# Local attention with a gated feed-forward network on one core: where Wo's weights stand in their slots, where raw weights land, and when the halo is zeroed

## The chip, the cores and the metric

The kernel runs on one core of a Trainium2 chip. The metric is the device time of one launch in microseconds, the median of several runs of the same build. A core has five engines that are named here as the profile names them: PE (matrix multiply, with PEld for its weight loads), DVE, ACT, POOL and SP. SP and POOL also issue the DMA transfers of this kernel.

## The reference, cut to what matters

One sequence of 2048 tokens with 640 features is layer-normalised to `xn`. Two branches are computed from `xn` and multiplied:

```
qkv  = xn @ wqkv                 # 640 -> 3 * 640, 32 heads of 20
o    = softmax(q . k over the tokens s, s-2, ..., s-14) . v
s    = o @ wo                    # 640 -> 640
g    = silu(silu(xn @ w1) @ w2)  # 640 -> 1536 -> 640
out  = x + s * g
```

Everything is float32.

## The kernel before, in words

**Groups.** The 2048 tokens are worked off in four groups of 512 (`NG` = 4, `T` = 4 tiles of `P` = 128 tokens). A group runs through `qkv_phase` (four quarters of the heads, each 3 x 160 columns), then, for the group before it, `wo_phase`, then `ffn_phase`. After the last group stands `wo_last`. The attention itself (`scores`, `values`) runs on DVE beside the matrix products of the phases that follow.

**Two halves of each number.** Each float32 operand is held as a rounded half and the rest (`TH`/`TL` for the normalised and transposed activations, `SH`/`SL` for the inner activations of the feed-forward network, `whi`/`wlo` for weights). A product is three passes: high by high, high by low, low by high. Each matmul takes one 128x128 stationary operand, loaded by a weight load of its own, and one moving operand:

- q, k, v (lines 633 to 635, and 579 for the first quarter): stationary `TH`/`TL`, moving 480 columns of a weight slot.
- w1 (lines 786 to 788): stationary 128 columns of a weight slot, moving 512 columns of `TH`/`TL`.
- w2 (lines 667 and 669, through `tm_mm`): stationary `SH`/`SL`, moving 384 and then 256 columns of a weight slot.
- Wo (the same lines 667 and 669, and 756 in `wo_last`): stationary `TH`/`TL` (which then hold the transposed attention output), moving 384 and then 256 columns of a weight slot.

**Weight slots.** `WR` has seven slots (`RING` = 7) of 2 x 640 numbers, that is 5120 bytes in each partition. The list `units` holds the 196 weight blocks in the order of use; block i goes to slot i mod 7. `start(u)` gives the first column of a block in its slot: 48 (`QAT`) for the blocks of wqkv and 0 for the others. The high half begins there and the low half 640 numbers (2560 bytes) further on. When PE is done with a block, `w_done` calls `w_load` for the block seven places on.

**First use and reuse.** The first time a block is needed its raw float32 weights are loaded by SP (`raw_load`, line 345; the very first load is issued by ACT), ACT rounds them into the high half (line 371), and DVE, or POOL for the first ones, computes the low half (line 374). The two halves are stored to DRAM (line 380), and later uses load both by one DMA that POOL issues (line 363). Of the 57 raw loads the first five land in `PR`, the next ones, in turn, in six places of 2560 bytes (two tiles `RAW` and four parts of the gate tile `G`), and those of group 1 in the two `RAW` tiles.

**Residual.** `wo_phase` loads the input rows again, into the two tiles `XR` (line 705, SP); POOL adds the gated attention to them (line 706), and SP stores the result (line 708).

**Halo.** Each quarter has a tile `KV[q]` with 7 extra positions for keys and values of neighbouring tokens. In group 0, POOL zeroes the first two partitions of these positions by a memset (line 641), before SP's shifting DMAs (line 454) fill the rest.

**Order.** Nothing is issued as it is written. `add` records each operation with its engine, an estimated duration, the keys that it reads and writes, and a priority; `Weave.order` then lays all operations out, PE's in the written order and the other engines' by readiness and priority, and emits them. Each engine works off its own list in that order; SP's and POOL's DMA issues wait in the same list.

**Placement.** The tiles stand in each partition in the order of allocation. In the built program `TH`, `TL` and all seven slots begin at the same place modulo 512 bytes (`TH[0]` at 17152, `TL[0]` at 37632, the slots from 58112 in steps of 5120, each 256 modulo 512). The small tile `ST[1]` stands between the slots and `SH`, so that `SH` and `SL` begin 64 bytes later modulo 512.

Of the kernel before, what the change touches and what calls it, by code (L numbers as in the profile page):

```python
# [9 lines left out]
F32R = mybir.dt.float32r  # L10
# [4 lines left out]
P = 128  # L15
S, D, F, H, DH = 2048, 640, 1536, 32, 20
# [12 lines left out]
CA, CB = 384, 256  # L29
RING = 7  # L30
# [2 lines left out]
LO = 10  # L33
BY_ACT = (0,)
QAT = 48
X_AT = 3, 7, 8
TILE_AT = 1, 1.5, 5, 6
LOW_AT = 3
# [20 lines left out]
class Weave:  # L59
# [19 lines left out]
    def add(self, eng, dur, fn, reads=(), writes=(), prio=0.0, lock=False, table=None, nbytes=0):  # L79
        o = Op()  # L80
        o.eng, o.dur, o.fn, o.prio, o.lock, o.table, o.nbytes = eng, dur, fn, prio, lock, table, nbytes
        o.seq, o.users, o.ready = len(self.ops), [], 0.0
        before = set()
        for k in reads:
            if k in self.writer:
                before.add(self.writer[k])
        for k in writes:
            if k in self.writer:
                before.add(self.writer[k])
            before.update(self.readers.get(k, ()))  # L90
        for k in writes:
            self.writer[k] = o
            self.readers[k] = []
        for k in reads:
            self.readers.setdefault(k, []).append(o)
        before.discard(o)
        o.left = len(before)
        for b in before:
            b.users.append(o)
        self.ops.append(o)  # L100
        return o
# [71 lines left out]
def local_attention_silu_ffn(ctx: ExitStack, tc: tile.TileContext, x, wqkv, wo, w1, w2, out):  # L173
# [19 lines left out]
    def tiles(name, n, shape, dtype=F32):  # L193
        return [sb.tile(shape, dtype, name=f"{name}{i}") for i in range(n)]
# [4 lines left out]
    ST = [sb.tile([P, 2, 6], F32, name="st0")]  # L199
    TH = tiles("th", 2, [P, DC, TOK], F32R)  # L200
    TL = tiles("tl", 2, [P, DC, TOK], F32R)
    WR = tiles("w", RING, [P, 2 * D], F32R)
    ST.append(sb.tile([P, 2, 6], F32, name="st1"))
    SH = tiles("sh", 2, [P, TOK], F32R)
    SL = tiles("sl", 2, [P, TOK], F32R)
# [11 lines left out]
    G = sb.tile([P, T, D], F32, name="gate")  # L217
    XR = tiles("xr", 2, [P, D])
    SF = tiles("sf", 2, [P, TOK])
    RAW = tiles("raw", 2, [P, D])  # L220
    ACC = [psum.tile([P, TOK], F32, name=f"acc{i}") for i in range(6)]
    ROT = [psum.tile([P, TOK], F32, name=f"rot{i}") for i in range(2)]
    carry = [dram.tile([2, NQ, 2, T, CQ], F32, name=f"carry{par}") for par in range(2)]
# [8 lines left out]
    def bank():  # L232
        i = take("acc", 6)
        return ACC[i], ("acc", i)
# [14 lines left out]
    def act(n, fn, reads, writes, prio, table=None):  # L249
        add("ACT", ac(n), fn, reads, writes, prio, table=table)  # L250
# [5 lines left out]
    def dma(fn, reads, writes, nbytes, prio, dur=0.45):  # L256
        add("SP", dur, fn, reads, writes, prio, nbytes=nbytes)
# [37 lines left out]
    def store_at(u):  # L295

        return 1 + (u[0] == "q" and u[2] % 2)

    for u in units:
        n = seen[u] = seen.get(u, 0) + 1  # L300
        at = store_at(u)
# [5 lines left out]
    def width(u):  # L307
        return 3 * CQ if u[0] == "q" else D

    def start(u):  # L310

        return QAT if u[0] == "q" else 0

    def raw_load(k):


        if k >= len(fresh):
            return
        i = fresh[k]
        u = units[i]  # L320
        n = width(u)
        if k < DC:
            r, kr = PR.rearrange("p t w m -> p (t w m)")[:, k * n:(k + 1) * n], [PRK[k]]
        elif k < early:
            s = (k - DC) % 6
            r, kr = (RAW[s], [("raw", s)]) if s < 2 else (G[:, s - 2, :], [("g", s - 2, 0), ("g", s - 2, CA)])
            r = r[:, :n]
        else:
            s = k % 2
            r, kr = RAW[s][:, :n], [("raw", s)]  # L330
        raws[i] = r, kr
        if u[0] == "q":
            _, q, c = u
            src = wqkv[c * P:(c + 1) * P, :].rearrange("p (s m) -> p s m", s=3)[:, :, q * CQ:(q + 1) * CQ]
            dst = r.rearrange("p (s m) -> p s m", s=3)
        elif u[0] == "w1":
            src = w1.rearrange("(c p) f -> p c f", p=P)[:, :, u[1] * P:(u[1] + 1) * P]
            dst = r.rearrange("p (c f) -> p c f", c=DC)
        else:
            m = wo if u[0] == "wo" else w2  # L340
            src, dst = m[u[1] * P:(u[1] + 1) * P, :], r
        if k in BY_ACT:
            add("ACT", 0.65, lambda: nc.scalar.dma_start(dst, src), [], kr, -1, nbytes=n * P * 4)
            return
        dma(lambda: nc.sync.dma_start(dst, src), [], kr, n * P * 4, 1 + k if k < 2 * DC else clock[0] + 5,
            0.62 if k < 2 * DC else 0.45)

    def w_load():
        i = loaded[0]
        if i >= len(units):  # L350
            return
        loaded[0] += 1
        u, s = units[i], i % RING
        n = width(u)
        r = WR[s]
        at = start(u)
        both = r.rearrange("p (s d) -> p s d", s=2)[:, :, at:at + n]
        whi, wlo = both[:, 0], both[:, 1]
        kh, kl = ("wh", s), ("wl", s)
        due = clock[0]  # L360
        if what[i] == "load":
            src = halves[u]
            add("POOL", 1.0, lambda: nc.gpsimd.dma_start(both, src), [("half", u)], [kh, kl], due + 10,  # L363
                nbytes=2 * n * P * 4)
            return
        k = fresh.index(i)
        if not k:
            raw_load(0)
            rawn[0] = 1
        raw, kr = raws.pop(i)  # L370
        act(n, lambda: nc.scalar.activation(whi, raw, AF.Copy), kr if k else kr + [("sd", 0)], [kh], 1000 + due)
        pool_does = k < LO and k not in ON_DVE
        eng, cost, by = ("POOL", po(n), nc.gpsimd) if pool_does else ("DVE", dv(n), nc.vector)
        add(eng, cost, lambda: by.tensor_tensor(
            out=wlo, in0=raw, in1=whi.bitcast(F32), op=OP.subtract), [kh] + kr, [kl],
            due if pool_does else LOW_AT if k < LO else 50, lock=True)
        if what[i] == "store":
            kept = dram.tile([P, 2, n], F32, name="half_" + "_".join(map(str, u)))
            halves[u] = kept
            dma(lambda: nc.sync.dma_start(kept, both.bitcast(F32)), [kh, kl], [("half", u)], 2 * n * P * 4,  # L380
                due + 25)
        while rawn[0] <= (min(k + 6, early - 1) if k < early - 2 else k + 2):
            raw_load(rawn[0])
            rawn[0] += 1

    def w_next(*want):
# [4 lines left out]
        s, n, at = i % RING, width(want), start(want)  # L391
        return WR[s][:, at:at + n], WR[s][:, D + at:D + at + n], ("wh", s), ("wl", s)

# [5 lines left out]
    def load_x(g, t, n=1, prio=None):  # L399
        dma(lambda: nc.sync.dma_start(XIN[:, t:t + n], rows(xg, g)[:, t:t + n]), [],  # L400
            [("xin", u) for u in range(t, t + n)], n * P * D * 4, clock[0] if prio is None else prio)
# [124 lines left out]
    def first_quarter(i):  # L526
# [59 lines left out]
        for k in range(2):  # L586
            cs = slice(k * 320, (k + 1) * 320)
            dma(lambda cs=cs: nc.sync.dma_start(XIN[:, 0, cs], rows(xg, 0)[:, 0, cs]), [],
                [("xin", 0) if k else ("xin", 0, "a")], P * 320 * 4, 0)
        for k, p in enumerate(X_AT):  # L590
            load_x(0, k + 1, prio=p)
# [27 lines left out]
    def qkv_phase(g, i, io):  # L619
        for q in range(NQ):  # L620
            if g == 0 and q == 0:
                ps = first_quarter(i)
            else:
                ps = [bank() for t in range(T)]
                for c in range(DC):
                    wh, wl, kh, kl = w_next("q", q, c)
                    for t in range(T):
                        o, kp = ps[t]

                        def unit(c=c, t=t, o=o, wh=wh, wl=wl):  # L630
                            o = o[:, :3 * CQ]
                            hi, lo = TH[i][:, c, tsl(t)], TL[i][:, c, tsl(t)]
                            nc.tensor.matmul(o, hi, wh, start=c == 0, stop=False)  # L633
                            nc.tensor.matmul(o, lo, wh, start=False, stop=False)  # L634
                            nc.tensor.matmul(o, hi, wl, start=False, stop=c == DC - 1)  # L635
                        pe(3 * mm(480), unit, t_keys(i, [c], [t]) + [kh, kl], [kp])
                    w_done()
                    if g and (q, c) in O_AT:
                        o_chunk(g - 1, O_AT[q, c], io)
            if g == 0:  # L640
                add("POOL", 2.0, lambda q=q: nc.gpsimd.memset(KV[q][0:2, :, 0:HALO, :], 0.0), ["first"] if q else [],
                    [("halo", q, 1, 0), ("halo", q, 2, 0), ("halo", q, 3, 0), ("halo", q, 4, 0)], 1 + q)
            for t in range(T):
                evac_qkv(g, q, t, *ps[t])
            halo(g, q)
            scores(g, q)
            if q:
                values(g, q - 1)
        values(g, NQ - 1)
# [217 lines left out]
```

## Time and profile before

| | |
|---|---|
| median of 3 runs | 642.76 us (641.28 to 643.1) |
| the profiled execution | 641.45 us |
| its span, first to last instruction | 639.6 us |
| PE busy | 632.7 us (99%) |
| DVE busy | 538.7 us (84%) |
| ACT busy | 207.2 us (32%) |
| POOL busy | 123.4 us (19%) |
| HBM read, written | 109.55 MB, 34.16 MB |

Busy times are those of the profiled execution. Matmuls overlap each other in the records, since one begins before the last rows of the one before it are out; what a matmul costs PE is therefore read from start to start in the timeline, and the duration of one record is longer than that.

### The profile page before, as it was taken

The numbers are of one execution on the slowest core, as the hardware profiler recorded it, in microseconds if no ns is written. First come the engines' busy times: TensorE is split into PE (matmuls) and PEld (weight loads), VectorE is DVE, ScalarE is ACT, GpSimd is POOL, SyncE is SP. The second block draws the span as 40 slices with busy tenths as digits, with TensorE's granted clock in tenths as the row PEclk, the third lists the DMA queues.
The fourth block names the chain that finished last, engine by engine and source line by source line (L and its number), as shares of the span: only waits on it lengthen the run. The fifth ranks groups of instructions, "written<-read, shape, count | busy, mean of one in ns | idle before, by whom it ended". The sixth has DMA issues, their size and how long they took to land.

```text
span 639.6 us, 9015 instructions
## 1 busy us (share of the span) xinstructions
PE 632.7 (99%) x3495; PEld 572.5 (90%) x3495; DVE 538.7 (84%) x539; ACT 207.2 (32%) x401; POOL 123.4 (19%) x168
## 2 busy tenths in 40 slices
PE   7999999999999999999999999999999999999997
PEld 6888889999889989999888999999988899899997
DVE  6699999999999989999839998999106999899814
ACT  4436453443534022324332112223313222233230
POOL 4500000001101241111222125111222213411100
PEclk9999999999999999999999999999999999999999
DMA  9999999777999998657699978865679995885522
GB/s 280 338 306 318 335 403 378 293 233 225 282 328 323 291 303 256 194 167 214 183 267 276 291 219 272 304 186 165 170 208 258 285 301 194 270 305 185 186 83 82
DMA packets 74154, 162.44 MB, mean 254 GB/s; under 512 B 5648, under 2 KB 47088, under 8 KB 74112
## 3 DMA queue, kind: packets, MB, share of 16 engines
q0 software_dynamic: 26672, 82.58, 44.9%
q1 hardware_dynamic: 47040, 79.05, 39.7%
q8 instruction: 27, 0.44, 0.3%
q10 hardware_dynamic: 400, 0.25, 0.1%
q14 instruction: 15, 0.12, 0.1%
HBM read 109.55 MB, written 34.16 MB: 225 GB/s over the span
## 4 chain that ended last, share of the span: by engine, by line
PE 98%; DVE 1%; DMA 1%; ACT 0%; issue 0%; SPq 0%
PE acc L667 22%; PE acc L669 15%; PE acc L633 10%; PE acc L634 10%; PE acc L635 10%; PE rot L788 9%; PE rot L786 9%; PE rot L787 9%; PE rot L429 2%; PE acc L579 2%; DMA xin<-in_A_x_dram 1%; PE rot L756 0%; DVE xin L549 0%; PE rot L558 0%; DVE st L544 0%; ACT th L562 0%
## 5 line engine op out<-in xcount | busy, mean ns | idle before, releaser
L633 PE MATMUL acc<-w,th 128*128 128x480 f32 x300 | 114.7, 382 | 0.0
L667 PE MATMUL acc<-w,sh 128*128 128x384 f32 x384 | 113.6, 335 | 0.0
L634 PE MATMUL acc<-w,tl 128*128 128x480 f32 x300 | 113.5, 378 | 0.0
L635 PE MATMUL acc<-w,th 128*128 128x480 f32 x300 | 113.4, 378 | 0.0
L669 PE MATMUL acc<-w,sh 128*128 128x256 f32 x384 | 107.1, 279 | 0.0
L477 DVE TENSOR_TENSOR pr<-q,kv 128x2560 f32<-128x2560 f32 x32 | 90.3, 2821 | 11.6 <-DMA kv<-kv 11.2
L786 PE MATMUL rot<-th,w 128*128 128x512 f32 x240 | 95.4, 398 | 0.0
L788 PE MATMUL rot<-th,w 128*128 128x512 f32 x240 | 94.0, 391 | 0.0
L787 PE MATMUL rot<-tl,w 128*128 128x512 f32 x240 | 93.9, 391 | 0.0
L509 DVE TENSOR_TENSOR pr<-e,kv 128x2560 f32<-128x2560 f32 x32 | 90.3, 2821 | 0.8
L480 DVE TENSOR_REDUCE l<-pr 128x128 f32<-128x2560 f32 x32 | 90.0, 2814 | 0.2
L363 POOL DMA_DIRECT2D w<-half_q x52 | 37.4, 719 | 233.3 <-DVE pr L514 93.5
L514 DVE TENSOR_TENSOR pr<-pr 128x1280 f32<-128x1280 f32 x64 | 76.6, 1197 | 1.1
L792 ACT ACTIVATE sh<-rot 128x512 fp32r<-128x512 f32 x48 | 28.8, 600 | 149.3 <-PE rot L788 146.6
L669 PEld LDWEIGHTS acc<-w,sh 128*128 128x128 f32 x384 | 72.3, 188 | 1.6
L667 PEld LDWEIGHTS acc<-w,sh 128*128 128x128 f32 x384 | 72.1, 188 | 1.7
L363 POOL DMA_DIRECT2D w<-half_w x72 | 38.6, 537 | 179.3 <-PE acc L669 96.4
L635 PEld LDWEIGHTS acc<-w,th 128*128 128x128 f32 x300 | 56.3, 188 | 8.5
L634 PEld LDWEIGHTS acc<-w,tl 128*128 128x128 f32 x300 | 56.4, 188 | 8.0
L633 PEld LDWEIGHTS acc<-w,th 128*128 128x128 f32 x300 | 56.3, 188 | 8.0
L667 PE MATMUL acc<-w,sl 128*128 128x384 f32 x192 | 57.8, 333 | 0.0
L434 DVE TENSOR_TENSOR tl<-rot,th 128x512 fp32r<-128x512 f32 x35 | 23.8, 681 | 38.3 <-ACT th L433 38.2
(88 smaller groups left out, 1002.9 us busy)
## 6 DMA issues: line engine op xcount, KB each, us to landing
w<-half_w POOLq DMA_DIRECT2D x72, 640.0 KB, 5.5
w<-half_q POOLq DMA_DIRECT2D x52, 480.0 KB, 5.1
half_w<-w SPq DMA_DIRECT2D x24, 640.0 KB
half_q<-w SPq DMA_DIRECT2D x20, 480.0 KB
w<-half_wo POOLq DMA_DIRECT2D x15, 640.0 KB, 5.4
kv<-kv SPq DMA_DIRECT2D x16, 560.0 KB
kv<-kv SPq DMA_DIRECT2D x16, 420.0 KB
gate<-in_B_w_dram SPq DMA_DIRECT2D x16, 320.0 KB
```

The costliest lines, as they stand in the source:

```text
L477: dve(2560, lambda t=t: nc.vector.tensor_tensor(out=PR, in0=win(qq[:, t:t + 2, :], W, 0), in1=win(kv[:, 0, t:t + 2, :], W, CQ), op=OP.mult ...
L480: dve(2560, lambda t=t: nc.vector.tensor_reduce(out=l[:, t:t + 2].rearrange("p t w h -> p (t w h)"), in_=PR.rearrange("p t w (h d) -> p (t ...
L509: dve(2560, lambda t=t, v=v: nc.vector.tensor_tensor(out=PR.rearrange("p t w (h d) -> p t (w h) d", d=DH), in0=e[:, t:t + 2].rearrange("p ...
L514: dve(2 * n * CQ, lambda n=n: nc.vector.tensor_tensor(out=PR[:, :, 0:n, :], in0=PR[:, :, 0:n, :], in1=PR[:, :, n:2 * n, :], op=OP.add), [] ...
L633: nc.tensor.matmul(o, hi, wh, start=c == 0, stop=False)
L634: nc.tensor.matmul(o, lo, wh, start=False, stop=False)
L635: nc.tensor.matmul(o, hi, wl, start=False, stop=c == DC - 1)
L667: nc.tensor.matmul(a[t][0][:, :CA], st, w[:, :CA], start=first, stop=last)
L669: nc.tensor.matmul(b[t // 2][0][:, h * CB:(h + 1) * CB], st, w[:, CA:], start=first and h == 0, stop=last, skip_group_check=True)
L786: nc.tensor.matmul(h, wh[:, cs], TH[i][:, c, :], start=c == 0, stop=False)
L787: nc.tensor.matmul(h, wh[:, cs], TL[i][:, c, :], start=False, stop=False)
L788: nc.tensor.matmul(h, wl[:, cs], TH[i][:, c, :], start=False, stop=c == DC - 1)
```

## The change

Three edits. The blocks of Wo begin 48 numbers (192 bytes) into their slots, as those of wqkv do already (`WOAT`). Since such a block needs 48 + 1280 numbers in a row, each slot becomes 64 numbers longer (`SLOT` = 1344 numbers, 5376 bytes), and the two halves are cut out of the slot from `at` on. To make room, the tiles `RAW` go, and the raw weights that landed in them land in the tiles `XR`. The memsets of the halo get the priorities 1, 13, 25 and 37 instead of 1, 2, 3 and 4.

In the built program the slots now begin at 58112 + 5376 i: those with an even number at 256 modulo 512 as before, those with an odd number at 0. `TH` and `TL` stay where they were, and `SH` and `SL` begin at 64 modulo 512. The number of instructions is the same. On SP the first two residual loads move from place 17 of its list to behind the splitting of Wo's weights in group 1, and on POOL the second and third memset change places with splits of weights (memset, split, memset, split, memset instead of three memsets and two splits).

```diff
+WOAT = 48
+SLOT = 2 * D + 64
...
-    WR = tiles("w", RING, [P, 2 * D], F32R)
+    WR = tiles("w", RING, [P, SLOT], F32R)
...
-    RAW = tiles("raw", 2, [P, D])
...
-        return QAT if u[0] == "q" else 0
+        return QAT if u[0] == "q" else WOAT if u[0] == "wo" else 0
...
-            r, kr = (RAW[s], [("raw", s)]) if s < 2 else (G[:, s - 2, :], [("g", s - 2, 0), ("g", s - 2, CA)])
+            r, kr = (XR[s], [("xr", s)]) if s < 2 else (G[:, s - 2, :], [("g", s - 2, 0), ("g", s - 2, CA)])
             r = r[:, :n]
         else:
             s = k % 2
-            r, kr = RAW[s][:, :n], [("raw", s)]
+            r, kr = XR[s][:, :n], [("xr", s)]
...
-        both = r.rearrange("p (s d) -> p s d", s=2)[:, :, at:at + n]
+        both = r[:, at:at + 2 * D].rearrange("p (s d) -> p s d", s=2)[:, :, :n]
...
                 add("POOL", 2.0, lambda q=q: nc.gpsimd.memset(KV[q][0:2, :, 0:HALO, :], 0.0), ["first"] if q else [],
-                    [("halo", q, 1, 0), ("halo", q, 2, 0), ("halo", q, 3, 0), ("halo", q, 4, 0)], 1 + q)
+                    [("halo", q, 1, 0), ("halo", q, 2, 0), ("halo", q, 3, 0), ("halo", q, 4, 0)], 1 + 12 * q)
```

## The prediction

> **What bounds the kernel now.** I read the page's first two parts and the clock first, then the chain, then PE's own waits.
>
> ```profile
> span 639.6 us, 9015 instructions
> PE 632.7 (99%) x3495; PEld 572.5 (90%) x3495; DVE 538.7 (84%) x539; ACT 207.2 (32%) x401; POOL 123.4 (19%) x168
> PE 98%; DVE 1%; DMA 1%; ACT 0%; issue 0%; SPq 0%
> ...
> core 0: 639.6 us, clock 0.999
> ...
> PE rot L558 <- DVE xin L549: 1.5, 2, 0.8
> PE rot L532 <- POOL ident masks.py:199: 1.4, 1, 1.4
> PE acc L579 <- DVE tl L566: 0.3, 1, 0.3
> ```
>
> PE is busy for 99% of the span at full granted clock, 98% of the chain is PE, and the three waits of PE (3.2 us together) belong to the transposes and the first quarter at the start. Nothing after that shows as a wait of PE. So the time moves in two ways only: a matmul takes a different time from start to start, or an engine that feeds PE comes late where it is in time today. The diff removes no instruction, so both must be read in the timeline.
>
> **Edit 1, Wo's start in its slot.** First the number of matmuls that it touches: 128x384 and 128x256 pairs that stream Wo against `TH` or `TL`, from the groups by form.
>
> ```profile
> L667 PE MATMUL acc<-w,th 128*128 128x384 f32 x160 | 48.9, 338 | 0.0
> L669 PE MATMUL acc<-w,th 128*128 128x256 f32 x150 | 42.2, 281 | 0.0
> L667 PE MATMUL acc<-w,tl 128*128 128x384 f32 x80 | 25.8, 338 | 0.0
> L669 PE MATMUL acc<-w,tl 128*128 128x256 f32 x75 | 21.0, 280 | 0.0
> L756 PE MATMUL rot<-w,th 128*128 128x256 f32 x10 | 1.4, 281 | 0.0
> L756 PE MATMUL rot<-w,tl 128*128 128x256 f32 x5 | 0.8, 282 | 0.0
> ```
>
> 160 + 80 = 240 matmuls of 384 columns, and 150 + 75 + 10 + 5 = 240 of 256: 240 pairs. Next, what a pair costs, from start to start in PE's timeline (first column the start). Wo, w2, q and w1 in that order:
>
> ```profile
> 203.07 0.34 PE L667 MATMUL acc<-w,th 128*128 128x384 f32 x1
> ...
> 219.80 0.39 PE L786 MATMUL rot<-th,w 128*128 128x512 f32 x1
> ...
> 98.39 0.33 PE L667 MATMUL acc<-w,sh 128*128 128x384 f32 x1
> 98.56 0.28 PE L669 MATMUL acc<-w,sh 128*128 128x256 f32 x1
> ...
> 100.97 0.40 PE L786 MATMUL rot<-th,w 128*128 128x512 f32 x1
> ...
> 186.23 0.38 PE L633 MATMUL acc<-w,th 128*128 128x480 f32 x1
> ...
> 190.12 0.37 PE L633 MATMUL acc<-w,th 128*128 128x480 f32 x1
> ...
> 96.83 0.39 PE L786 MATMUL rot<-th,w 128*128 128x512 f32 x1
> ...
> 97.51 0.34 PE L667 MATMUL acc<-w,sh 128*128 128x384 f32 x1
> ...
> 101.67 0.39 PE L786 MATMUL rot<-th,w 128*128 128x512 f32 x1
> ```
>
> From 203.07 the last 57 pairs of the first Wo phase run to 219.80: 16.73 / 57 = 293.5 ns a pair. From 98.39 nine pairs of w2 run to 100.97: 2.58 / 9 = 286.7 ns. The shapes are the same, the weight loads are as many, and PE waits in neither. What differs is where the two operands stand. Call lead the start of the moving operand less that of the stationary one, modulo 512 bytes (tiles and halves step by multiples of 512, so one lead holds for a whole phase). Before, Wo has lead 0; w2 has lead -64, that is 448, since `SH` stands 64 bytes on; q has 192 through `QAT`; w1 has 0. After, Wo has lead 192 in slots with an even number and 448 in the others: modulo 256 it is always 192, which is w2's lead too.
>
> The nearest row for the changed pair is therefore w2's: same shapes, same lead modulo 256. At its price Wo saves 6.8 ns a pair, 240 x 6.8 = 1.63 us, all of it on the path, since PE has no slack. The other end comes from q, which has lead 192 against the very same `TH`: 18 matmuls from 186.23 to 190.12, 3.89 / 18 = 216.1 ns. Of a w2 pair the 384 columns take 0.17 us (98.39 to 98.56) and the 256 the other 0.117, which is some 0.42 ns a column and 8 ns for each matmul; 480 columns would take 211 by that line, and q takes 5 more. If Wo's matmuls lost as much at this lead, a pair would take 286.7 + 10 = 296.7, and Wo would lose 3.2 x 240 = 0.8 us. So the edit is worth between -1.6 and +0.8 us. I take -1.6, since shape decides how two streams meet, and w2 has Wo's.
>
> [...]
>
> **Edit 1's other half, the longer slots.** They move what nobody meant to move. Slots with an odd number now begin 256 bytes off modulo 512. Blocks go round the seven slots, so of w2's 48 blocks 20 lie in even slots and get lead 192 instead of 448, of q's 80 blocks 33 in odd slots get 448 instead of 192, and of w1's 48 blocks 12 get 256 instead of 0. If only the lead modulo 256 counts, none of this costs anything. If modulo 512 counts, q's and w2's prices change places: w2 loses 20 x 12 pairs x 10 ns = 2.4 us, q gains 33 x 12 matmuls x 5 ns = 2.0 us, Wo's blocks gain 6.8 in 11 odd slots and lose 3.2 in 9 even ones (12 pairs each: -0.9 + 0.3), and w1 is open: its steady step is (97.51 - 96.83) / 3 = 227 ns and its first steps in a block (101.67 - 100.97) / 3 = 233, so 12 x 15 matmuls cost between 0 and 6 ns more, 0 to 1.1 us. That sums to -0.2, or +0.9 with w1. I take 0, by the same reason as above.
>
> **Edit 2, raw weights in `XR`.** The number of landing places stays six in group 0 and two in group 1, so raw loads are no later. What waits anew is the first pair of residual loads: they must now stand behind the last raw block of Wo.
>
> ```profile
> 16.71 1.17 SPq L705 DMA_DIRECT2D xr<-in_A_x_dram  x2
> ...
> 208.73 0.34 SPq L380 DMA_DIRECT2D half_wo<-w  x1
> ...
> 225.57 6.47 SPq L705 DMA_DIRECT2D xr<-in_A_x_dram  x2
> ...
> 220.77 1.56 POOL L706 TENSOR_TENSOR xr<-xr,gate 128x640 f32<-128x640 f32 x1 [3.50 <-DVE gate L699]
> 222.54 0.57 POOL L363 DMA_DIRECT2D w<-half_w  x1 [0.20 <-issue]
> 236.85 1.57 POOL L706 TENSOR_TENSOR xr<-xr,gate 128x640 f32<-128x640 f32 x1 [0.74 <-DMA xr<-in_A_x_dram]
> ...
> 240.88 0.53 POOL L363 DMA_DIRECT2D w<-half_w  x1 [1.94 <-PE rot L788]
> 244.33 0.53 POOL L363 DMA_DIRECT2D w<-half_w  x1 [2.92 <-PE acc L669]
> w<-half_w POOLq DMA_DIRECT2D x72, 640.0 KB, 5.5
> ```
>
> Today they are issued at 16.71. In the new list the later of the two follows the store at 208.73, so it leaves SP at about 209.1. The second pair tells how long such a load takes: issued by 232.04 (225.57 + 6.47), landed when the add starts at 236.85, 5 us. So the data is there by 214, and POOL's add at 220.77, which waits for DVE's gate anyway, waits no longer. Behind it in POOL's list stand the weight loads. A slot is refilled every 3.45 us (244.33 - 240.88) and read six blocks later, 20.7 us, and a load lands in 5.5: about 15 us are left even if the add came late. Price 0. SP is spared the two early issues (1.17 us); PE waits for nothing there, so that is worth nothing either.
>
> **Edit 3, the memsets.** Here is the one place after the start where PE is nearly late.
>
> ```profile
> 24.81 5.79 POOL L641 MEMSET kv<- 2x2240 f32 x3
> 30.57 2.83 POOL L374 TENSOR_TENSOR w<-gate,w 128x480 fp32r<-128x480 f32 x2
> 31.98 0.38 PE L633 MATMUL acc<-w,th 128*128 128x480 f32 x1
> ```
>
> The three memsets hold POOL for 5.79 us. The two splits behind them end at 33.40, the first of them half of 2.83 after 30.57, so at about 32.0; it writes the weights of the block that PE begins at 31.98. The margin is 0.2 us or less. With one memset ahead instead of three this split ends 3.9 us earlier and the next 1.9 us earlier. In the profiled execution that saves nothing, since PE did not wait. In a slower start it saves what POOL was late. The median of the runs shown lies 1.3 us above the profiled execution (642.76 against 641.45), and how much of that is this place no row shows; bounds 0 and 1.3. I take 0.6. The last memset now ends when today's second split does, 33.4; its quarter is the fourth, whose matmuls begin two quarters of 60 x 216 ns, 26 us, after the second's: no cost.
>
> **The sum.** The profiled execution: 641.45 - 1.6 = 639.8, a span of 638.0. For the median: 642.76 - 1.6 - 0.6 = 640.6 us, 0.34% less. A measurement of this kernel can tell about 0.3%, 1.9 us, from no change, so the forecast stands near that edge.
>
> **The rivals.**
> *q gains too.* Odd slots give q w2's lead, and if that alone counts its 33 blocks save up to 2.0 us more, with w2 losing nothing: 638.6. Against it: w2 would have to be indifferent to a lead that hurts q. 10%.
> *The lead is not the cause.* Wo differs from w2 also in passing through `TH` and `TL` in turn, and its slower pairs may come from there, or it takes q's excess. Then Wo gives 0 to +0.8, and 642.76 - 0.6 + 0.4 = 642.6. [...] 16%.
> *Modulo 512.* Prices change places as summed above, -0.2 to +0.9, with the margin of edit 3: 642.5. 8%.
> *The longer slots spoil w2 and w1.* The other side: w2's 20 blocks lose their lead (+2.4), w1's 12 blocks stay at their first steps (+1.1), q and Wo's even slots get nothing back, Wo's odd slots gain 0.9: +2.6 and, where POOL's margin brought nothing, 645.4. It decides if the period is 512 bytes and a difference of 256 is bad for 512-column streams. For it: q's extra 5 ns at 192. Against it: three pairs of w2 from 97.51 to 98.39, the first in their block, take 293 ns each before the rest settle at 287, so the lead is not all that counts. 12%.
> *A queue.* If the second residual load landed more than 6 us later than reckoned, POOL's add would wait, and past another 15 us PE would. Each us beyond is a us. SP's list is fuller at that place by one issue. Say 645. 6%.
>
> **How the numbers follow.** 48% for the forecast, of which 5 fall within 0.3% because edit 3 may bring nothing. Faster by over 0.3%: 43 + 10 = 53%. Within: 5 + 16 + 8 = 29%. Slower: 12 + 6 = 18%. The range reaches below q's gain (638.6) to 638.4, and above through the two cases near 642.6 and part of the spoiled slots to 644.0; about 2 in 10 lie outside.
>
> **What would show it.** Right: in the timeline Wo's pairs at about 287 ns, w2's still at 287, q's matmuls at 216, w1's at 227 whatever the slot; POOL's split of the fourth block of the second quarter done by 28.5; POOL's first residual add still released by DVE. Wrong: Wo's pairs at 293 or more in even slots, w2's pairs or w1's steps that differ by slot, or any wait of PE past 20 us for POOL or for a weight load.

## The result, and the profile after

The changed kernel takes 643.77 us in the median of 14 runs (642.75 to 644.38), the kernel before 642.47 us in 14 runs on the same chip (641.28 to 643.83). The ratio is 1.002, interval 1.0012 to 1.0027: slower by 1.3 us. The prediction had said 640.6 and 53% for faster. The value lies inside its range of 638.4 to 644.0, near the upper end, because that range was wide; the sign is wrong. The profiled execution took 644.09 us, its span 642.3 us, against 641.45 and 639.6 before.

From the page after, and from the clock by core:

```profile
span 642.3 us, 9024 instructions
PE 635.4 (99%) x3495; PEld 575.1 (90%) x3495; DVE 538.4 (84%) x539; ACT 207.0 (32%) x401; POOL 123.9 (19%) x168
...
core 0: 642.3 us, clock 0.997
```

PE's busy time grew by 2.7 us (632.7 to 635.4), as much as the span; PE has as many matmuls as before, and the other engines are within 0.6 us. So no engine came late: matmuls became longer. PE's own waits after are the old ones at the start:

```profile
PE rot L559 <- DVE xin L550: 1.4, 2, 0.8
...
PE acc L580 <- DVE tl L567: 0.3, 1, 0.3
```

Which matmuls grew shows in the groups by form (all lines are one further on than before; the second number behind the bar is the mean ns of one record):

```profile
L668 PE MATMUL acc<-w,th 128*128 128x384 f32 x160 | 49.7, 342 | 0.0
L670 PE MATMUL acc<-w,th 128*128 128x256 f32 x150 | 42.7, 285 | 0.0
```

Before, these two rows had 48.9 us at 338 ns and 42.2 at 281. A record of 384 columns after lasts 0.34 us, and the next one begins 0.18 us after its start (217.38 behind 217.20). So, from start to start in PE's timeline after (first column the start): Wo in slots of both kinds, then w2, q and w1 at the places that the prediction read.

```profile
217.20 0.34 PE L668 MATMUL acc<-w,th 128*128 128x384 f32 x1
...
220.20 0.34 PE L668 MATMUL acc<-w,tl 128*128 128x384 f32 x1
...
99.62 0.33 PE L668 MATMUL acc<-w,sh 128*128 128x384 f32 x1
...
101.34 0.33 PE L668 MATMUL acc<-w,sl 128*128 128x384 f32 x1
...
188.75 0.38 PE L634 MATMUL acc<-w,th 128*128 128x480 f32 x1
...
192.64 0.38 PE L634 MATMUL acc<-w,th 128*128 128x480 f32 x1
...
97.38 0.39 PE L787 MATMUL rot<-th,w 128*128 128x512 f32 x1
98.06 0.39 PE L787 MATMUL rot<-th,w 128*128 128x512 f32 x1
```

Wo: ten pairs in 3.00 us, 300.0 ns a pair against 293.5 before. w2: six pairs in 1.72 us, still 286.7. q: 18 matmuls in 3.89 us, still 216.1. w1: three in 0.68 us, still 227. Summed over all matmuls, from each start to the next, the Wo matmuls of 384 columns gained 1.23 us, those of 256 gained 0.19 and the separate ones at the end lost 0.06, in all +1.36; q behind its first quarter, w1 and w2 differ as wholes by 0.07 us or less from before. Those 1.36 us account for the 1.3 us of the medians.

The profiled executions differ by 2.7 us because that of after also met a lower granted clock at the start: its first quarter's 60 matmuls (line 580) took 15.80 us from start to start, against 14.31. Busy time by stretch (engines, then PEclk, DMA share, GB/s), after and then before:

```profile
core 0: us, PE busy (x) PEld busy (x) DVE busy (x) ACT busy (x) POOL busy (x), PEclk, DMA share, GB/s
8.00:10.00 2.00, 1.74 (x8) 1.30 (x7) 1.96 (x8) 1.85 (x5) 0.68 (x1) 0.70 1.11 346
10.00:12.00 2.00, 2.00 (x7) 1.65 (x6) 1.72 (x4) 0.68 (x2) 1.24 (x1) 0.50 1.09 338
```

```profile
10.00:12.00 2.00, 2.00 (x13) 1.65 (x11) 1.94 (x6) 1.22 (x3) 0.93 (x1) 1.00 1.08 345
```

At half clock PE began 7 matmuls in those 2 us instead of 13. This is not the change's doing: executions of both kernels come with and without it, and by the mean clock they fall into two groups. After: 6 executions at 1.0 took 642.75 to 643.48, 8 at 0.996 or 0.997 took 643.75 to 644.38. Before, in the runs beside two of the experiments: 8 at 0.999 or 1.0 took 641.17 to 642.13, 11 at 0.996 or 0.997 took 642.35 to 642.82. Within either group after lies some 1.7 us above before, though these were not run side by side. Beside another experiment (after_nudge_best) the two groups of before overlap, 641.25 to 642.83 and 642.25 to 643.42, with medians of 642.14 and 642.86: the clock goes with most of the spread, not with all of it.

### The profile page after: what moved, and what is told of

Same layout as the page of the kernel before. It is cut to its first block, busy times and chain, and to the rows that moved or that the text cites. A ratio compares the mean times of both kernels' runs of the same rounds, so it can differ in the third digit from the quotient of the medians.

```text
span 642.3 us, 9024 instructions
## 1 busy us (share of the span) xinstructions
PE 635.4 (99%) x3495; PEld 575.1 (90%) x3495; DVE 538.4 (84%) x539; ACT 207.0 (32%) x401; POOL 123.9 (19%) x168
## 4 chain that ended last, share of the span: by engine, by line
PE 98%; DVE 1%; DMA 1%; ACT 0%; issue 0%; SPq 0%
PE acc L668 22%; PE acc L670 15%; PE acc L635 10%; PE acc L634 10%; PE acc L636 10%; PE rot L789 9%; PE rot L787 9%; PE rot L788 9%; PE rot L430 2%; PE acc L580 2%; DMA xin<-in_A_x_dram 1%; PE rot L757 0%; DVE xin L550 0%; PE rot L559 0%; DVE st L545 0%; ACT th L563 0%
```

## The experiments

**The one edit undone: Wo's start.** Longer slots, raw weights in `XR` and the later memsets stay.

```diff
-WOAT = 48
+WOAT = 0
```

> The change without its first edit: Wo's blocks start at 0 of their (still longer) slots. If Wo's start alone made the changed kernel slower: Wo's pairs go back from 300.0 to 293.5 ns, 240 x 6.5 = 1.6 us, and the time goes back to that of the kernel before, 642.5 within 0.3. Rival, the longer slots or the shared tiles cost something that the rates do not show: the time stays at 643.2 or above although Wo's pairs are back. Rival, edit 3 brings something: below 642.1.

Measured: 642.5 us in 11 runs (641.86 to 643.3), ratio 1.0001, interval 0.9992 to 1.001. In its timeline 14 pairs of Wo take 4.10 us, 293 ns a pair as before:

```profile
213.70 0.34 PE L668 MATMUL acc<-w,tl 128*128 128x384 f32 x1
...
217.80 0.34 PE L668 MATMUL acc<-w,th 128*128 128x384 f32 x1
```

So Wo's start is the whole cost. The other two edits and the longer slots together bring and cost nothing that can be measured; this run does not separate them.

**Other starts.** One start for all blocks (0, 64, 128 or 192 bytes into the slot, for q, Wo, w1 and w2 alike), Wo alone at 128 bytes, and `TH` and `TL` moved 64 bytes on with Wo's blocks back at 0 (a tile of 64 bytes before `TH` and one of 192 before the slots).

```diff
     def start(u):
-        return QAT if u[0] == "q" else WOAT if u[0] == "wo" else 0
+        return 16        # all_at_16; 0, 32 and 48 in the others
```
```diff
-WOAT = 48
+WOAT = 32                # wo_at_32; 0 in th_at_64
+    PAD = [sb.tile([P, 16], F32, name="pad0")]       # th_at_64, before TH
+    PAD.append(sb.tile([P, 48], F32, name="pad1"))   # th_at_64, before WR
```

> All blocks, those of wqkv too, start at 0. If q loses 5 ns a matmul through its start at 192 bytes (as Wo lost 6.5 ns a pair by the same step), q falls from 216 to about 212 and the time by 960 x 4 = 3.8 us. If the start at 192 is good for 480 columns and bad for 384 and 256, q rises above 216: Wo at 0 lies 6 ns over w2 a pair, so some 3 to 6 ns a matmul, 3 to 6 us.

> All blocks start 64 bytes into their slots. If the lead (moving start less stationary start, modulo 256) decides whatever the operands, w2 (now lead 0) takes what Wo took at lead 0, 293.5 ns a pair, and Wo and q (lead 64) take the same price per matmul as each other. If the moving operand's own start decides, w2, Wo and q all change alike, and w1, whose moving operand stays, keeps 227. If the stationary operand's own start decides, w1 changes alone.

> All blocks start 128 bytes into their slots. Lead: w2 gets 64, Wo and q 128, w1 128. By the lead w2 takes here what Wo takes at 64 bytes. By the moving operand's own start the three change alike again and w1 keeps 227 ns; if only 128-byte lines count, all rates are those of the start at 0.

> All blocks 192 bytes into their slots: q and Wo as in the changed kernel (216 ns, 300 ns a pair), so w2 and w1 are what is new. w2 has moving 192 and stationary 64, a lead of 128, at which Wo was fastest (286.7 or less a pair expected by the lead). If the moving operand's own start decides, w2 is at its worst here, 293 or more. w1 has lead 64; by the lead it takes some ns more than 227 as it did at 64 and 128 bytes (233, 232).

> The changed kernel with Wo's blocks 128 bytes into their slots instead of 192. With all blocks at 128 bytes Wo's 384 columns took 169.7 ns on average instead of 176.8 at 0 and 181.9 at 192. If Wo's cost goes by its own start alone and not by its neighbours: Wo gains 1.5 us against the kernel before, all else as before, 641.0 against 642.5. Rival, the rate at 128 bytes came from w2 and q standing there too (the state in which they leave PE): Wo stays at 293 or more a pair and the time at 642.5.

> Wo's blocks at 0 of their slots, and the four tiles TH and TL moved by 64 bytes, so that Wo has just w2's starts modulo 256: moving 0, stationary 64. If the two starts modulo 256 decide the price of a pair, Wo takes w2's 286.7 ns instead of 293.5 and gains 1.6 us. Rival, the alternation of TH and TL or another difference of the phases: Wo stays at 293.5 or above. q (moving 192, stationary 64) and w1 (moving 64, stationary 0) move too; by the two starts w1 takes what Wo took at moving 64 and stationary 0, little more than at 0.

Measured, in one execution each but for wo_at_32: all_at_0 642.76 us, all_at_16 650.3, all_at_32 649.07, all_at_48 644.72, th_at_64 649.56; wo_at_32 641.19 in 12 runs (640.24 to 642.56), ratio 0.9985, interval 0.9976 to 0.9993. The rates, each from PE's timeline. First all_at_16 (w2), then all_at_32 (w2, Wo), ten pairs between the two rows of each:

```profile
99.60 0.34 PE L668 MATMUL acc<-w,sh 128*128 128x384 f32 x1
...
102.53 0.34 PE L668 MATMUL acc<-w,sl 128*128 128x384 f32 x1
```

```profile
99.93 0.34 PE L668 MATMUL acc<-w,sh 128*128 128x384 f32 x1
...
102.87 0.34 PE L668 MATMUL acc<-w,sl 128*128 128x384 f32 x1
...
215.23 0.33 PE L668 MATMUL acc<-w,tl 128*128 128x384 f32 x1
...
218.09 0.33 PE L668 MATMUL acc<-w,th 128*128 128x384 f32 x1
```

w2 takes 2.93 and 2.94 us for ten pairs, some 293 ns a pair, where it had 286.7; Wo at 128 bytes takes 2.86. Two kernels show two rates at one lead. In all_at_48 the third w2 block runs ten pairs in 2.87 us, the fourth three pairs in 0.90; in th_at_64 the first Wo phase runs ten pairs in 2.87 us, the second in 3.00:

```profile
84.11 0.33 PE L668 MATMUL acc<-w,sh 128*128 128x384 f32 x1
...
86.98 0.33 PE L668 MATMUL acc<-w,sl 128*128 128x384 f32 x1
...
91.58 0.34 PE L668 MATMUL acc<-w,sh 128*128 128x384 f32 x1
...
92.48 0.34 PE L668 MATMUL acc<-w,sh 128*128 128x384 f32 x1
```

```profile
217.97 0.33 PE L670 MATMUL acc<-w,tl 128*128 128x384 f32 x1
...
220.84 0.33 PE L670 MATMUL acc<-w,th 128*128 128x384 f32 x1
...
374.97 0.34 PE L670 MATMUL acc<-w,th 128*128 128x384 f32 x1
...
377.97 0.34 PE L670 MATMUL acc<-w,tl 128*128 128x384 f32 x1
```

The two phases of th_at_64 have the same slots, the same starts modulo 512 bytes and the same shapes, though the first reads `TH[0]` and the second `TH[1]`. Its first w2 block in the second group and that in the third have the same slot and the same stationary tile, and run at 300.0 and 286.7. And wo_at_32, with 128 bytes, shows 287 ns in its first phase (also in the second and third) and 300 in the last:

```profile
214.92 0.33 PE L668 MATMUL acc<-w,th 128*128 128x384 f32 x1
...
217.79 0.33 PE L668 MATMUL acc<-w,th 128*128 128x384 f32 x1
...
622.11 0.34 PE L668 MATMUL acc<-w,th 128*128 128x384 f32 x1
...
625.11 0.34 PE L668 MATMUL acc<-w,tl 128*128 128x384 f32 x1
```

Put in order by lead modulo 256 bytes (moving less stationary), from the last six pairs of every block of Wo and w2:

| lead (bytes) | seen in | ns a pair |
|---|---|---|
| 0 | Wo before, wo_at_0, all_at_0; w2 in all_at_16 | 293 |
| 64 | Wo in all_at_16; w2 in all_at_32 | 293 |
| 128 | Wo in wo_at_32, all_at_32; w2 in all_at_48 | 286.7 or 300.0 |
| 192 | w2 before and after; Wo after, all_at_48; both in th_at_64 | 286.7 or 300.0 |

Other values stand only in blocks that are changing over. In th_at_64 w2 has the lead and the start in the slot that it has before, and half of its blocks run at 300. In these executions, then, the lead decides whether there is one rate or a choice of two, and something else decides the choice. For q and w1 (sums over 900 and 720 matmuls, less those of before): q costs +0.62 us with lead 0 (all_at_0), +1.95 with 64, +2.36 with 128, against the 192 it has; w1 costs +3.13 us with 192 (all_at_16), +2.61 with 128 (all_at_32) and +0.94 with 64 (all_at_48), against the 0 it has. Both stand best where they are. The two outcomes named for q in all_at_0, some 3 to 6 us of gain or of loss, both missed. What makes all_at_16, all_at_32 and th_at_64 so slow is q and w1 at worse leads and w2, which costs +3.2, +3.0 and +3.5 us more there.

**The entry alone.** The moment at which a run of such pairs begins is called its entry here. An extra matmul ahead of each Wo phase of the changed kernel, into the accumulator that the next one clears. No address moves.

```diff
+                    if c == 0 and t == 0:
+                        n = (256, 264, 272)[g]      # after_nudge_b: 260, 304, 336
+                        nc.tensor.matmul(a[0][0][:, :n], TH[i][:, 0, tsl(0)], wh[:, :n], start=True, stop=True)
                     tm_mm(banks, t, TH[i][:, c, tsl(t)], wh, c == 0, False)
...
         def whole(t, cols):
+            n = (258, 288, 320, 0)[t]               # after_nudge_b: 128, 352, 384
+            if n:
+                nc.tensor.matmul(a[t][0][:, :n], TH[i][:, 0, tsl(t)], ws[0][0][:, :n], start=True, stop=True)
```

> The changed kernel with one more matmul ahead of each Wo phase, into the accumulator that the next matmul clears: 256, 264 and 272 columns ahead of the first three phases, and in the last phase 258, 288 and 320 ahead of its first, second and third run of 15 pairs. No address changes. Theory A, two steady states: at a lead of 128 or 192 bytes (modulo 256) a pair runs at 286.7 or at 300.0 ns, the state is picked by the moment at which the stream begins, and holds until something interrupts it. Then some of the six entries fall to 286.7, none shows 293.3 throughout; a phase of 60 pairs that changes state gains 60 x 13.3 = 0.8 us, a run of 15 pairs 0.2 us. Theory B, the addresses fix the price: 300.0 after every entry, and the six matmuls make the kernel 0.8 us longer than the changed one.

> As the one before, with other lengths: 260, 304 and 336 columns ahead of the first three Wo phases, 128, 352 and 384 ahead of the first three runs of 15 pairs in the last. Theory A: some entries at 286.7 ns a pair, others at 300.0, and a length that gives 286.7 can be kept for a faster kernel. Theory B: 300.0 everywhere.

Measured: 641.49 and 643.38 us. In after_nudge_a, the extra matmul and ten pairs of the first phase, then of the second:

```profile
201.78 0.28 PE L695 MATMUL acc<-w,th 128*128 128x256 f32 x1
...
213.93 0.34 PE L668 MATMUL acc<-w,th 128*128 128x384 f32 x1
...
216.93 0.34 PE L668 MATMUL acc<-w,th 128*128 128x384 f32 x1
...
359.15 0.28 PE L695 MATMUL acc<-w,th 128*128 128x264 f32 x1
...
371.07 0.33 PE L668 MATMUL acc<-w,tl 128*128 128x384 f32 x1
...
373.94 0.33 PE L668 MATMUL acc<-w,th 128*128 128x384 f32 x1
```

After 256 columns 3.00 us, after 264 columns 2.87 us. Over both kernels 264, 272, 288, 336, 128 and 384 columns left the pairs at 286.7, and 256, 258, 260, 304, 320 and 352 at 300.0; inside the last phase one extra matmul turned 300.0 into 286.7 (288 columns) and the next turned it back (320). A rate, once taken, held for the rest of the phase, over five blocks and slots of both kinds. The addresses are those of the changed kernel, so they do not fix the price: there is a choice of two.

**Lengths kept.** 272 columns ahead of the first three phases and 128 ahead of the last; the second kernel also has 25 dummy transposes at the start.

```diff
-                        n = (256, 264, 272)[g]
+                        n = (272, 272, 272)[g]
-            n = (258, 288, 320, 0)[t]
+            n = (128, 0, 0, 0)[t]
-WARM, WARM2 = 20, 3
+WARM, WARM2 = 25, 3      # the second kernel only
```

> The changed kernel with the extra matmul at the lengths that gave 286.7 ns: 272 columns ahead of the first three Wo phases, 128 ahead of the last phase, none inside it. Theory A (two states, picked at the entry): all 240 pairs at 286.7 instead of 300.0, 3.2 us off the changed kernel's 642.75 to 644.38, some 640.3 to 640.6 in the median, about 0.3% under the kernel before. If the lengths worked by chance of timing that differs from execution to execution, the times spread between 640 and 644.

> The same with 25 dummy transposes at the start instead of 20. Theory A with the clock that holds at the start: wo_at_32_warm_25's 640.25 less 0.8 us for the last phase, whose 60 pairs ran at 300.0 there, so about 639.5, ratio 0.9955, and a spread of some 0.3 us. Theory B for the last phase (it stays at 300.0 when the first three do not): 640.3.

Measured: 641.15 us in 11 runs (639.74 to 642.82), ratio 0.9976, interval 0.9966 to 0.9986; and 640.65 in 6 (639.83 to 641.53), ratio 0.9967, interval 0.9955 to 0.9979. These are 0.7 and 1.1 us above what was expected of all pairs at 286.7, and the trace of the first says why. Its first and third phase, which have the same slots, the same `TH` and `TL` and the same extra matmul of 272 columns; ten pairs each, the extra matmul shown for the first:

```profile
201.86 0.29 PE L695 MATMUL acc<-w,th 128*128 128x272 f32 x1
...
210.92 0.33 PE L668 MATMUL acc<-w,th 128*128 128x384 f32 x1
...
213.78 0.33 PE L668 MATMUL acc<-w,tl 128*128 128x384 f32 x1
...
517.18 0.34 PE L668 MATMUL acc<-w,th 128*128 128x384 f32 x1
...
520.18 0.34 PE L668 MATMUL acc<-w,th 128*128 128x384 f32 x1
```

The same length, 2.86 us and then 3.00; the second phase runs at 300.0 too. In after_nudge_a the third phase also had 272 columns ahead of it, at the same addresses, and ten of its pairs took 2.86 us:

```profile
517.31 0.33 PE L668 MATMUL acc<-w,th 128*128 128x384 f32 x1
...
520.17 0.33 PE L668 MATMUL acc<-w,th 128*128 128x384 f32 x1
```

So neither the addresses nor the length of the extra matmul fixes the rate. In the second kernel, where the clock at the start no longer adds its own spread, the six times are 639.83 twice, 640.64, 640.66 and 640.70, and 641.53: steps of some 0.8 us, and one phase of 60 pairs at the other rate is 60 x 13.3 ns = 0.8 us. Its profiled execution (640.66) has one of the four phases at 300.0. The steps suggest that the rate of a phase differs between executions of one program; only one execution of it has a trace. The miss is that the length is not a safe handle.

**The best version.** Wo at 128 bytes, where the first three phases ran at 286.7 unaided; then more dummy transposes; then an extra matmul ahead of the last phase.

```diff
-WOAT = 48
+WOAT = 32
-WARM, WARM2 = 20, 3
+WARM, WARM2 = 25, 3
+            n = (128, 0, 0, 0)[t]     # in whole(); last_three: 288, 352, 384
```

> The same with 25 instead of 20 transposes of the identity at the start. Before, executions at a mean granted clock of 0.999 to 1.0 took 641.3 to 641.9 and those at 0.997 took 642.5 to 643.3; in the profile of the changed kernel the clock is 0.70 and 0.50 between 8 and 12 us. If PE's idle us from 5.5 to 6.7 is what lets the clock fall, five more transposes fill it, the share of executions at 0.997 falls and the median by up to 1.2 us against the kernel at 128 bytes. Rival: the later gaps of PE (0.9 and 0.7 us, waiting for the normalised rows and their halves) are enough, and nothing changes; or the transposes end too late and the first quarter starts up to 1 us later.

> wo_at_32_warm_25 with one more matmul of 128 columns ahead of the last Wo phase, none elsewhere. Its first three phases ran at 286.7 ns a pair without help, the last at 300.0. Theory A (two states, picked at the entry, at a lead of 128 as at 192): the last phase enters at 286.7, 0.8 us less than 640.25 less the 0.06 us of the matmul, about 639.5, with a spread of some 0.3 us since nothing else varies. Theory A with the length wrong for this lead: 640.3. Theory B (the last phase's price at this start is fixed): 640.3 in every execution.

> wo_at_32_warm_25 with 288, 352 and 384 columns ahead of the first three runs of 15 pairs in the last phase. Theory A: the runs differ, some at 286.7 and some at 300.0 ns a pair, 0.2 us for each that changes. Theory B: 300.0 in all of them.

Measured: wo_at_32_warm_25 640.25 us in 7 runs (640.22 to 640.5), ratio 0.9974, interval 0.9964 to 0.9985. All 19 executions of kernels with 25 transposes, those of the next two and of the second kernel above included, had a clock of 0.999 or 1.0. Of PE's waits in this kernel the row for the transposes of `xin` has one wait of 0.7 us where it had two, 1.5 us together before:

```profile
PE rot L559 <- DVE xin L550: 0.7, 1, 0.7
```

wo_at_32_last_128 takes 639.82 us in 5 runs (639.65 to 639.95), ratio 0.9958, interval 0.9945 to 0.9972: 0.4% faster than the kernel before, and the fastest of all. Its last phase runs at 286.7 throughout. It gained 0.43 us, not the 0.74 that was expected: of the last phase's matmuls only 45 are pairs (45 x 13.3 ns = 0.6 us; the other 15 of each width run apart), and the entry costs some 0.1 us. wo_at_32_last_three took 640.84 us, with all three runs of the last phase at 300.0 after 288, 352 and 384 columns. That is Theory B's result in that kernel; wo_at_32_last_128 beside it, at the same addresses, rules B out.

## Why the prediction was wrong

**What bounds the kernel: right.** PE stayed busy for 99% of the span, and it has no new wait. The time moved in the first of the two ways named, matmuls that take another time from start to start.

**Edit 1, Wo's start: the step that failed.** The step read "shape decides how two streams meet, and w2 has Wo's", which was an assumption that no row showed, took w2's row as the nearest and gave -1.6 us. Measured: +6.6 ns a pair, +1.36 us. The other end, drawn from q's row, had the right sign but was too small (296.7 ns and +0.8 us against 300.0 and +1.36). What the runs showed in its place: at w2's lead a pair has two rates, 286.7 and 300.0 ns; w2 takes the first in 47 of its 48 blocks before and after, and Wo fell into the second. Taking the lead modulo 256 as the quantity that counts was right, as the table by lead shows; taking one row as the price of a lead was not. Calling the end at +0.8 a bound was the second fault. Its sum is also off: at the prediction's own 0.42 ns a column and 8 ns a matmul, 480 columns take 209.6 ns and not 211, which makes q's excess 6.5 ns, a pair 299.7 and the end +1.5 us. That this comes close to what was measured is luck, since the sum knows nothing of two rates, and starts shown to 0.01 us do not fix such a line to some ns. The trace of before held the second rate, in a place that was not read: its last w2 block, ten pairs between these rows of its timeline, with the same lead and slots as the others.

```profile
614.89 0.34 PE L667 MATMUL acc<-w,sh 128*128 128x384 f32 x1
...
617.89 0.34 PE L667 MATMUL acc<-w,sl 128*128 128x384 f32 x1
```

3.00 us, 300.0 ns a pair. In the other three groups the last w2 block follows the one before it without a break and runs at 286.7; here transposes stand between the two. Had all 48 blocks of w2 been read instead of one, the term could have been put at "either -1.6 or +1.6", and the forecast at no change.

**The longer slots: right.** Price 0: in the changed kernel Wo and w2 run at the same rate in odd and even slots (w2's last block apart, which runs at 300.0 before and after), and q and w1 cost what they did before. The rivals "q gains too", "modulo 512" and "the longer slots spoil w2 and w1" fall with that.

**Edit 2, raw weights in `XR`: price right, two details wrong.** The later of the two residual loads left SP by 210.97, near the forecast 209.1, but was not there "by 214", and POOL's first add waited for a residual load, not for DVE's gate:

```profile
224.40 1.56 POOL L707 TENSOR_TENSOR xr<-xr,gate 128x640 f32<-128x640 f32 x1 [5.61 <-DMA xr<-in_A_x_dram]
```

It began 3.6 us later than before (220.77), 1.2 of them because this execution runs late since the start, and held POOL's weight loads up. If it waited for the later load, that one took some 13 us where the second pair's row had suggested 5. The 15 us of slack that the prediction named as cover took it, and wo_at_0, which keeps this edit, has ratio 1.0001. "A queue" was the right place to look: the first of its two conditions came true, the load more than 6 us late, and the second, another 15 us, did not.

**Edit 3, the memsets: the gain of 0.6 us was not there.** POOL's order is what the diff says:

```profile
24.87 1.23 POOL L375 TENSOR_TENSOR w<-gate,w 128x480 fp32r<-128x480 f32 x1 [9.31 <-ACT w L372]
26.04 1.97 POOL L642 MEMSET kv<- 2x2240 f32 x1
27.98 1.23 POOL L375 TENSOR_TENSOR w<-gate,w 128x480 fp32r<-128x480 f32 x1
```

The split of the fourth block ends at 29.2, 2.8 us earlier than the old 32.0, although this execution runs 1.2 us late since the start (24.87 against 23.64 for the first of these splits); less that delay it is 28.0, as "done by 28.5" had it. The prediction guessed from the 1.3 us between the median and the profiled execution that PE waited there in slower executions. Most of those 1.3 us go with the clock at the start, as the two groups above show. That PE never waits there in any execution is not shown; wo_at_0, which keeps this edit too, shows no gain.

By microsecond, the clock in the changed kernel's trace is 0.89 from 8 to 9 us, 0.50 in each of the next three and 0.90 from 12 to 13: 1.7 us of clock lost, which is 3.4 us at half. PE's longest wait in it is 1.4 us. The trace of before has the same longest wait and a clock of 1.00 from 8 to 14 us. What lets the clock fall in some executions and not in others, no run here shows; with 25 transposes at the start instead of 20 the mean clock was 0.999 or 1.0 in all 19.

**The rivals.** "The lead is not the cause" had, in Wo taking q's excess, the right sign for this term. Its first half, a cost of passing through `TH` and `TL` in turn, falls: Wo does so at 286.7, 293 and 300.0 ns a pair, by start and entry.

**Still open:** what in the chip makes two rates, and what at the entry picks one. The lengths that worked show no rule, and the same length gave both rates. So it is also open why Wo took 300.0 in all four phases of the changed kernel's trace, and 286.7 in three of four at 128 bytes.

## What to carry to other kernels

Before a row is used as the price of a stream, read the same stream in all its blocks: a price that takes two values may come out as either after a change next to it. Test an expected gain from placement by moving that one start through all its values; here 0, 128 and 192 bytes gave 642.5, 641.2 and 643.8 us. And split the executions by granted clock before a gap between median and profile is put down to an engine.

## What the runs showed of the hardware that was not expected

- A stream of pairs (384 and 256 columns, float32 halves, a weight load for each) repeated at 286.7, 293 or 300.0 ns. Leads of 0 and 64 bytes modulo 256 gave 293; leads of 128 and 192 gave one of the other two, which from the seventh pair on held to the end of a Wo phase of 45 or 60 pairs wherever nothing stood in between.
- Behind one extra matmul, of 0.12 us at 272 columns, a phase of 60 pairs at unchanged addresses ran at either rate, 13.3 ns a pair apart.
- With no wait of PE above 1.4 us at the start, the changed kernel's trace has half clock for some 3.4 us. A mean clock below 0.999 was met in 68 of the 115 executions with 20 dummy transposes whose clock is on record, and in none of the 19 with 25.
